# V's range and four copies of transposed probabilities on VectorE; the accumulators of the feed-forward layer copied out by ScalarE and VectorE in turn, earlier in the engines' order

## The chip, the cores and the metric

The kernel runs on one core of a Trainium2 chip. A core has five engines with instruction queues of their own: TensorE (PE; its weight loads are shown apart as PEld), VectorE (DVE), ScalarE (ACT), GpSimd (POOL) and SyncE (SP), which here issues all the DMAs. Each engine works through its queue in order and waits on semaphores for the others. SBUF is the on-chip memory; PSUM is the memory that matmuls write to. The metric is the device time of one execution in microseconds (us), given as the median of several runs.

## The reference

```python
scores = q @ k.T / sqrt(64)                      # B=4, H=8, S=768, D=64
scores += -slopes[h] * dist                      # slopes 2**-(h+1)
scores = where(keep, scores, -1e9)               # 8 global columns, or the 96 last keys
a = exp(scores - max); a /= a.sum() + 1e-9
x = (a @ v).transpose(0, 2, 1, 3).reshape(3072, 512)
h = x @ moe_w_in                                 # 512 x 2048
g = maximum(h, 0) + alpha * minimum(h, 0)        # alpha: one per column of h
out = g @ moe_w_out                              # 2048 x 512
```

q, k and v arrive as fp32, the two weight matrices as 64-bit floats; out is fp32.

## The kernel before

**Units.** The 3072 tokens are cut into 12 units of 256 tokens, three to a batch (unit u belongs to batch u // 3). `attend(u, h)` does one head of a unit: scores sp on PE, bias and maximum on DVE (pr and sm, L670), exp on ACT (L675), then the probabilities are transposed. In units 0 to 2 PE transposes them into PSUM (tp, L696) and ACT copies them to SBUF (pt, L700); in later units a DMA does it (ps to vp's layout, L720). `av` (L734) multiplies with V, and DVE writes the normalised head into xn (L743). `x_transpose` makes xt, the feed-forward layer's input, as a high and a low half-precision part.

**Feed-forward layer.** Each unit goes through 16 blocks f of 128 hidden columns. `ff_in` does h (12 matmuls of 128x256, L793), ACT scales it with alpha into g (L342), DVE takes the maximum (L814), ACT casts to the high part (L816), and POOL or DVE makes the low rest (L366). `ff_out` adds the block to two accumulators in PSUM, o_0 and o_1, 128 tokens each (3 matmuls of 128x512 for either, L831); from unit 2 on these come from a pool of two, so that the next unit's first o product into an accumulator waits until this one is emptied. After block 15 each is copied to SBUF with a scale: `os`, on ACT (L838), 128x512, and sent out by a DMA on SP (L841). Names carry the unit first: os6_1 is unit 6's second accumulator.

**V's range.** V is scaled by a power of two per batch. `v_range(b)` finds it: the batch's V is loaded in pieces (vr), the sum of absolute values of each row of 512 goes into a column of vm (6 columns; ACT, L446, one Abs with an accumulator for each 512), their maximum into vmm (L452), vdg = identity times vmm (L456), a matmul against ones spreads it over the partitions (vrow, L458), DVE takes the maximum (L460), and nine tiny instructions (L465 to L475) make vs (V's scale), vden and osc (the scale of os). For batch 0 the vr are loaded in three pieces of two rows (L438), for batches 1 to 3 in six (L444), through the two buffers of the tag "stage", which os uses too. vp, V as high and low part, is V times vs (L343 or L345 on first part, L367 on the rest), made from the loaded unit `raw`; raw's buffer is free for the next load after that.

**Weights.** In the first 125 us the weights of the 16 blocks are converted from 64-bit words and split (`wf`, `wb`, `whl`; L531 to L540 and L367), largely on DVE.

**Order.** Nothing is ordered by hand. Each operation is recorded with a key (for a block: its time slot; 16 a unit), one or more engines that may do it, with a cost in ns, and the buffers that it reads and writes. A list scheduler then plays the run through: an engine that comes free takes the ready operation of the lowest key whose buffers can be had, and an operation with several possible engines goes to a second one when the first is far behind. Buffers of one tag are handed out in the order of the keys of their first use, so one that stands later in this queue waits for those ahead of it even if a buffer is free. The tags that matter here: stage (2 buffers), wf (4), raw's four tags, o (2, PSUM). The queues that come out of it are fixed in the program.

Of the kernel before, what the change touches and what calls it, by code (L numbers as in the profile page):

```python
# [19 lines left out]
ALU = mybir.AluOpType  # L20
AX = mybir.AxisListType
PSUM = bass.MemoryType.PSUM

P = 128
# [6 lines left out]
NU = 12  # L31
# [255 lines left out]
def c_dma(nbytes):  # L287
    return nbytes / 360.0
# [5 lines left out]
VR = -23  # L294
# [28 lines left out]
def fast(tc, cn, a):  # L323
    nc = tc.nc
    ctx = ExitStack()
    with ctx:
# [7 lines left out]
        def op(eng, key, cost, fn, r=(), w=()):  # L334
            plan.op(key, r, w, (eng, cost, fn))
# [95 lines left out]
        def v_range(b, key):  # L431
            m = buf("vm", f"vm{b}", [P, 6])
            for i in range(3):

                t = [buf("w", f"vr{b}_{i}", [P, 2, 512])] * 2 if not b else [
                    buf("stage", f"vr{b}_{i}_{j}", [P, 512]) for j in range(2)]
                if not b:
                    op("SP", key, c_dma(P * 4096), lambda t=t, i=i: nc.sync.dma_start(  # L438
                        out=t[0].t, in_=a["v"][b, 2 * i : 2 * i + 2].rearrange("j p d -> p j d")), w=[t[0]])
                for j in range(2):  # L440
                    k = key + 2 * i + j if b else VR
                    x = (lambda t=t, j=j: t[j].t) if b else (lambda t=t, j=j: t[j].t[:, j, :])
                    if b:
                        op("SP", k, c_dma(P * 2048), lambda x=x, i=i, j=j: nc.sync.dma_start(  # L444
                            out=x(), in_=a["v"][b, 2 * i + j]), w=[t[j]])
                    op("ACT", k, c_act(512, ptr=1), lambda x=x, i=i, j=j: nc.scalar.activation(  # L446
                        out=x(), in_=x(), func=AF.Abs, accum_out=m.t[:, 2 * i + j : 2 * i + j + 1]),
                       r=[], w=[(t[j], j), (m, 2 * i + j)])
# [134 lines left out]
        def attend(u, h, key):  # L583
# [106 lines left out]
            if plain:  # L690
                tp = buf("ax" if u == 1 else idle(u, h, "av", "o", "o"), "tp" + uh, [P, 512])

                def transposes():
# [3 lines left out]

                op("PE", key + 2, 109 * nb, transposes, r=[pr], w=[tp])
                pt = buf(idle(u, h, "pt", "ps"), "pt" + uh, [P, 512])
                op("ACT", key + 2, c_act(npr, True), lambda: nc.scalar.copy(out=pt.t[:, :npr], in_=tp.t[:, :npr]),  # L700
                   r=[tp], w=[pt])
                prods = lambda: ((pt.t, vrt()),)
                used = [pt, rv]
                cost = 207 * nb
# [115 lines left out]
        def ff_out(u, f, key):  # L820
            gh, gl, parts = mo.pop((u, f))
            w = whl[f]
            if f == 0:
                acc[u] = [buf(("sp", "ax")[t] if u == 1 else "o", f"o{u}_{t}", [P, 512]) for t in range(2)]
            for t in range(2):
                o = acc[u][t]

                def products(t=t, o=o):
                    tok = slice(128 * t, 128 * t + 128)
                    for n, (g_, wi) in enumerate(((gh, 0), (gh, 1), (gl, 0))):  # L830
                        nc.tensor.matmul(o.t, lhsT=g_()[:, tok], rhs=w.t[:, wi, 512:1024],  # L831
                                         start=f == 0 and n == 0, stop=f == NF - 1 and n == 2)

                op("PE", key + 0.1 * t, 3 * 215.8, products, r=[*parts, (w, 1), (w, 3)], w=[o])
                if f == NF - 1:
                    s = buf("stage", f"os{u}_{t}", [P, 512])
                    by = osc[u // 3]
                    op("ACT", key, c_act(512, True, 1), lambda o=o, s=s, by=by: nc.scalar.mul(  # L838
                        out=s.t, in_=o.t, mul=by.t), r=[o, by], w=[s])
                    rows = u * UT + 128 * t  # L840
                    op("SP", key, c_dma(P * 2048), lambda s=s, rows=rows: nc.sync.dma_start(  # L841
                        out=a["out"][rows : rows + 128, :], in_=s.t), r=[s])

        def warm(key):

# [196 lines left out]
```

## Time and profile before

| what | value |
|---|---|
| runs | 657.33 us median of 3 (656.55 to 657.67) |
| profiled execution | 654.4 us, of which the span from the first to the last instruction is 652.6 |
| PE busy | 622.7 us, 95% |
| DVE busy | 516.0 us, 79% |
| ACT busy | 407.1 us, 62% |
| POOL busy | 167.6 us, 26% |
| mean granted PE clock | 0.998 |

PE and PEld overlap, and a busy PE need not be at its peak. The profile's rows give the start in us, the length in us, then engine, line and operation, the tile that is written, `<-`, and what is read, shapes as partitions x elements, and how many instructions follow one another; in square brackets the idle time of the engine just before, and what ended it. Rows of groups give busy time in us, mean ns of one, and idle time. Rows of waits give the total in us, how many there were, and the longest.

### The profile page before, as it was taken

The numbers are of one execution on the slowest core, as the hardware profiler recorded it, in microseconds if no ns is written. First come the engines' busy times: TensorE is split into PE (matmuls) and PEld (weight loads), VectorE is DVE, ScalarE is ACT, GpSimd is POOL, SyncE is SP. The second block draws the span as 40 slices with busy tenths as digits, with TensorE's granted clock in tenths as the row PEclk, the third lists the DMA queues.
The fourth block names the chain that finished last, engine by engine and source line by source line (L and its number), as shares of the span: only waits on it lengthen the run. The fifth ranks groups of instructions, "written<-read, shape, count | busy, mean of one in ns | idle before, by whom it ended". The sixth has DMA issues, their size and how long they took to land.

```text
span 652.6 us, 13802 instructions
## 1 busy us (share of the span) xinstructions
PE 622.7 (95%) x4940; PEld 442.4 (68%) x4940; DVE 516.0 (79%) x1422; ACT 407.1 (62%) x1093; POOL 167.6 (26%) x201
## 2 busy tenths in 40 slices
PE   8898989899999999899899999999999999999996
PEld 6675667576667776677677677677676777776663
DVE  6899999969779979868979878868979878844331
ACT  6897767565557666766566655675566665743432
POOL 0013434203324324303434123211532212200000
PEclk9999999999999999999999999999999999999999
DMA  8998422217546846655556566574657566311001
GB/s 298 402 408 328 138 83 83 83 35 173 174 100 124 196 110 125 168 148 139 138 144 140 152 139 140 140 164 110 171 152 135 133 162 138 84 33 33 34 1 37
DMA packets 115804, 92.86 MB, mean 142 GB/s; under 512 B 93968, under 2 KB 93968, under 8 KB 115728
## 3 DMA queue, kind: packets, MB, share of 16 engines
q1 hardware_dynamic: 115728, 91.91, 52.7%
q8 instruction: 40, 0.66, 0.4%
q14 instruction: 36, 0.29, 0.1%
HBM read 63.06 MB, written 6.29 MB: 106 GB/s over the span
## 4 chain that ended last, share of the span: by engine, by line
PE 43%; DVE 36%; DMA 9%; ACT 7%; issue 4%; POOL 0%; SPq 0%; DVEq 0%; ACTq 0%; POOLq 0%
PE o L831 18%; PE h L793 17%; DMA raw<-in_qkv_dram 8%; DVE ps L367 4%; PE sp L664 4%; DVE g L814 3%; DVE wf L537 3%; DVE wb L534 3%; DVE whl L367 3%; PE av L734 3%; DVE pr L670 3%; DVE vp L367 2%; ACT pr L675 2%; DVE wb L531 2%; DVE q L366 1%
## 5 line engine op out<-in xcount | busy, mean ns | idle before, releaser
L793 PE MATMUL h<-xt,whl 128*128 128x256 f16 x2304 | 281.7, 273 | 3.7 <-DVE g L814 2.1
L793 PEld LDWEIGHTS <-whl 128*128 128x128 f16 x2304 | 224.6, 98 | 65.6 <-issue 4.8
L831 PE MATMUL o<-whl,g 128*128 128x512 f16 x864 | 215.3, 380 | 5.1 <-ACT os L838 5.1
L831 PEld LDWEIGHTS <-g 128*128 128x128 f16 x864 | 77.8, 98 | 73.3 <-issue 7.0
L342 ACT ACTIVATE g<-h,ak 128x256 f32<-128x256 f32 x172 | 80.2, 467 | 56.7 <-PE h L793 55.4
L675 ACT ACTIVATE pr<-pr,sm 128x256 f32<-128x256 f32 (+1 forms) x192 | 93.1, 486 | 32.8 <-DVE sm L670 32.7
L814 DVE SCALAR_TENSOR_TENSOR g<-h,g 128x256 f32<-128x256 f32 x192 | 80.0, 418 | 34.9 <-ACT g L342 34.5
L816 ACT CAST g<-g 128x256 f16<-128x256 f32 x144 | 57.4, 399 | 77.1 <-DVE g L814 76.9
L670 DVE CUSTOM_DVE_ANT_0 pr<-sp,D 128x256 f32<-128x256 f32 (+1 forms) x192 | 71.5, 393 | 14.0 <-PE sp L664 13.5
L366 POOL TENSOR_TENSOR g<-g 128x256 f16<-128x256 f32 x58 | 44.3, 763 | 149.0 <-ACT g L816 141.1
L367 DVE SCALAR_TENSOR_TENSOR ps<-pr,ps 128x512 f16<-128x512 f32 (+1 forms) x72 | 61.1, 849 | 7.7 <-ACT ps L342 7.1
L366 DVE TENSOR_TENSOR g<-g 128x256 f16<-128x256 f32 x86 | 38.6, 448 | 26.1 <-ACT g L816 26.0
L366 POOL TENSOR_TENSOR gl<-g,gh 128x256 f16<-128x256 f32 x32 | 31.9, 998 | 104.6 <-ACT gh L816 94.3
L831 PE MATMUL o<-whl,gh 128*128 128x512 f16 x192 | 57.2, 380 | 0.0
L366 POOL TENSOR_TENSOR k<-raw,k 128x416 fp32r<-128x416 f32 (+1 forms) x37 | 41.0, 1108 | 52.9 <-ACT k L354 30.8
L366 POOL TENSOR_TENSOR q<-raw,q 64x256 fp32r<-64x256 f32 x42 | 34.0, 810 | 79.9 <-ACT q L354 57.8
L664 PE MATMUL sp<-k,q 128*128 128x256 f32 (+1 forms) x288 | 51.5, 301 | 2.5 <-DVE sm L670 1.6
L664 PEld LDWEIGHTS sp<-k,q 128*128 128x128 f32 x288 | 38.6, 190 | 4.9 <-issue 2.0
L367 DVE SCALAR_TENSOR_TENSOR vp<-raw,vs,vp 128x256 f16<-128x256 f32 (+1 forms) x72 | 40.7, 586 | 0.0
L831 PE MATMUL o<-whl,gl 128*128 128x512 f16 x96 | 36.4, 379 | 2.2 <-POOL gl L366 1.7
L675 ACT ACTIVATION_READ_ACCUMULATOR pr<-pr,sm 128x1 f32 x192 | 36.2, 188 | 0.0
L342 ACT ACTIVATE ps<-pr 128x512 f16<-128x512 f32 (+1 forms) x53 | 32.0, 604 | 1.4
(109 smaller groups left out, 696.0 us busy)
## 6 DMA issues: line engine op xcount, KB each, us to landing
raw<-in_qkv_dram SPq DMA_DIRECT2D x56, 464.0 KB, 3.9
w<-in_w_dram SPq DMA_DIRECT2D x32, 512.0 KB, 9.0
raw<-in_qkv_dram SPq DMA_DIRECT2D x24, 368.0 KB, 3.7
out_dram<-os SPq DMA_DIRECT2D x24, 256.0 KB, 2.3
vr<-in_v_dram SPq DMA_DIRECT2D x18, 256.0 KB, 3.8
first<-in_first_dram SPq DMA_DIRECT2D x4, 464.0 KB, 6.1
vr<-in_v_dram SPq DMA_DIRECT2D x3, 512.0 KB, 9.3
first<-in_first_dram SPq DMA_DIRECT2D x4, 336.0 KB, 9.5
```

The lines of the kernel that those rows point to most:

```text
L342: lambda: nc.scalar.mul(out=out(), in_=src(), mul=by.t if tile_ else by)),
L366: return e.tensor_tensor(out=out(), in0=src(), in1=hi(), op=ALU.subtract)
L367: return e.scalar_tensor_tensor(out=out(), in0=src(), scalar=val(), in1=hi(), op0=ALU.mult, op1=ALU.subtract)
L534: op("DVE", k, c_dve(n), lambda bits=bits, hi_=hi_: v.scalar_tensor_tensor(out=bits.t, in0=hi_(), scalar=-0x80000000, in1=bits.t, op0=ALU. ...
L537: op("DVE", k, c_dve(n), lambda w=w, bits=bits, lo_=lo_: v.scalar_tensor_tensor(out=w.t.bitcast(I32), in0=lo_(), scalar=29, in1=bits.t, op ...
L664: nc.tensor.matmul(sp.t[:, pc : pc + n], lhsT=q_()[:, 128 * qb : 128 * qb + 128], rhs=kk()[:, off : off + n], start=j == 0, stop=j == len( ...
L670: op("DVE", key, c_dve(n) + 10, lambda qb=qb, n=n, dc=dc, pc=pc: v.tensor_tensor_reduce(out=pr.t[:, pc : pc + n], in0=sp.t[:, pc : pc + n] ...
L675: op("ACT", key + 1, c_act(n, ptr=1) + 93, lambda qb=qb, n=n, pc=pc: nc.scalar.activation(out=pr.t[:, pc : pc + n], in_=pr.t[:, pc : pc + ...
L793: nc.tensor.matmul(hp.t, lhsT=w.t[:, wi, wc], rhs=x.t[:, NC * xi + c, :], start=n == 0, stop=n == 3 * NC - 1)
L814: op("DVE", key, c_dve(UT), lambda: v.scalar_tensor_tensor(out=g_(), in0=hp.t, scalar=KG, in1=g_(), op0=ALU.mult, op1=ALU.max), r=[hp], w= ...
L816: op("ACT", key, c_act(UT), lambda: nc.scalar.copy(out=gh_(), in_=g_()), r=[rg], w=[rh])
L831: nc.tensor.matmul(o.t, lhsT=g_()[:, tok], rhs=w.t[:, wi, 512:1024], start=f == 0 and n == 0, stop=f == NF - 1 and n == 2)
```

## The change

1. For batch 0 three DVE `tensor_reduce` with absolute value take the place of six ACT Abs: each reduces a loaded piece 128 x 2 x 512 into two columns of vm.
2. In unit 0, heads 4 to 7, the pt copy (128x384) is DVE's `tensor_copy` instead of ACT's.
3. os of o_0 stays on ACT, os of o_1 goes to DVE (`tensor_scalar`, 128x512 from PSUM); from unit 2 on both have a key lower by 8, eight blocks further up, and take a buffer of the tag wf instead of stage. The DMA keeps its key.
4. In unit 11, the last, each accumulator is copied in halves of 256 columns, the first by ACT and the second by DVE, with a DMA for each half.

```diff
@@ -437,12 +437,16 @@
                 if not b:
                     op("SP", key, c_dma(P * 4096), lambda t=t, i=i: nc.sync.dma_start(
                         out=t[0].t, in_=a["v"][b, 2 * i : 2 * i + 2].rearrange("j p d -> p j d")), w=[t[0]])
+                if not b:
+                    op("DVE", VR, c_dve(1024), lambda t=t, i=i: v.tensor_reduce(
+                        out=m.t[:, 2 * i : 2 * i + 2], in_=t[0].t, axis=AX.X, op=ALU.add, apply_absolute_value=True),
+                       r=[t[0]], w=[(m, i)])
+                    continue
                 for j in range(2):
-                    k = key + 2 * i + j if b else VR
-                    x = (lambda t=t, j=j: t[j].t) if b else (lambda t=t, j=j: t[j].t[:, j, :])
-                    if b:
-                        op("SP", k, c_dma(P * 2048), lambda x=x, i=i, j=j: nc.sync.dma_start(
-                            out=x(), in_=a["v"][b, 2 * i + j]), w=[t[j]])
+                    k = key + 2 * i + j
+                    x = lambda t=t, j=j: t[j].t
+                    op("SP", k, c_dma(P * 2048), lambda x=x, i=i, j=j: nc.sync.dma_start(
+                        out=x(), in_=a["v"][b, 2 * i + j]), w=[t[j]])
                     op("ACT", k, c_act(512, ptr=1), lambda x=x, i=i, j=j: nc.scalar.activation(
                         out=x(), in_=x(), func=AF.Abs, accum_out=m.t[:, 2 * i + j : 2 * i + j + 1]),
                        r=[], w=[(t[j], j), (m, 2 * i + j)])
@@ -697,8 +701,12 @@
 
                 op("PE", key + 2, 109 * nb, transposes, r=[pr], w=[tp])
                 pt = buf(idle(u, h, "pt", "ps"), "pt" + uh, [P, 512])
-                op("ACT", key + 2, c_act(npr, True), lambda: nc.scalar.copy(out=pt.t[:, :npr], in_=tp.t[:, :npr]),
-                   r=[tp], w=[pt])
+                if u == 0 and h >= 4:
+                    op("DVE", key + 2, c_dve(npr), lambda: v.tensor_copy(out=pt.t[:, :npr], in_=tp.t[:, :npr]),
+                       r=[tp], w=[pt])
+                else:
+                    op("ACT", key + 2, c_act(npr, True), lambda: nc.scalar.copy(out=pt.t[:, :npr], in_=tp.t[:, :npr]),
+                       r=[tp], w=[pt])
                 prods = lambda: ((pt.t, vrt()),)
                 used = [pt, rv]
                 cost = 207 * nb
@@ -833,13 +841,21 @@
 
                 op("PE", key + 0.1 * t, 3 * 215.8, products, r=[*parts, (w, 1), (w, 3)], w=[o])
                 if f == NF - 1:
-                    s = buf("stage", f"os{u}_{t}", [P, 512])
+                    s = buf("wf" if u > 1 else "stage", f"os{u}_{t}", [P, 512])
                     by = osc[u // 3]
-                    op("ACT", key, c_act(512, True, 1), lambda o=o, s=s, by=by: nc.scalar.mul(
-                        out=s.t, in_=o.t, mul=by.t), r=[o, by], w=[s])
                     rows = u * UT + 128 * t
-                    op("SP", key, c_dma(P * 2048), lambda s=s, rows=rows: nc.sync.dma_start(
-                        out=a["out"][rows : rows + 128, :], in_=s.t), r=[s])
+
+                    halves = (("ACT", 0, 256), ("DVE", 256, 512)) if u == NU - 1 else ((("ACT", "DVE")[t], 0, 512),)
+                    for e, lo, hi in halves:
+                        if e == "ACT":
+                            op("ACT", key - (8 if u > 1 else 0), c_act(hi - lo, True, 1), lambda o=o, s=s, by=by, lo=lo, hi=hi: nc.scalar.mul(
+                                out=s.t[:, lo:hi], in_=o.t[:, lo:hi], mul=by.t), r=[o, by], w=[(s, lo)])
+                        else:
+                            op("DVE", key - (8 if u > 1 else 0), c_dve(hi - lo, False, 1), lambda o=o, s=s, by=by, lo=lo, hi=hi: v.tensor_scalar(
+                                out=s.t[:, lo:hi], in0=o.t[:, lo:hi], scalar1=by.t, scalar2=None, op0=ALU.mult),
+                                r=[o, by], w=[(s, lo)])
+                        op("SP", key, c_dma(P * 4 * (hi - lo)), lambda s=s, rows=rows, lo=lo, hi=hi: nc.sync.dma_start(
+                            out=a["out"][rows : rows + 128, lo:hi], in_=s.t[:, lo:hi]), r=[(s, lo)])
 
         def warm(key):
 
```

Since the scheduler plays the whole run through with these operations, others change place and engine too. Up to the last weight split DVE's queue has, beside the new instructions, two 128x288 k rests fewer (POOL does them), one wf conversion fewer, two gl rests and one g more. The line numbers of the change are 4 to 16 higher than before.

The first place is DVE in unit 0, around the normalising of heads 0 to 3 (xn). Before:

```order
L684 RECIPROCAL sm0_2_267<-sm0_2_267 128x4
L743 TENSOR_TENSOR xn0_342<-av0_0_319,sm0_0_247 128x2x128
L670 ISA pr0_6_357,sm0_6_358<-sp0_6_346,D6_236 128x128
L670 ISA sm0_6_358 128x1
L670 ISA pr0_6_357,sm0_6_358<-sp0_6_346,D6_236 128x256
L670 ISA sm0_6_358 128x1
L670 ISA pr0_7_375,sm0_6_358<-sp0_7_354,D7_238 128x128
```

With the change:

```order
L441 TENSOR_REDUCE vm0_342<-vr0_0_215 128x2
L751 TENSOR_TENSOR xn0_360<-av0_0_319,sm0_0_247 128x2x128
L674 ISA pr0_6_369,sm0_6_370<-sp0_6_346,D6_236 128x128
L674 ISA sm0_6_370 128x1
L674 ISA pr0_6_369,sm0_6_370<-sp0_6_346,D6_236 128x256
L674 ISA sm0_6_370 128x1
L441 TENSOR_REDUCE vm0_342<-vr0_1_223 128x2
L751 TENSOR_TENSOR xn0_360<-av0_2_362,sm0_2_267 128x2x128
L705 COPY pt0_4_388<-tp0_4_378 128x384
L441 TENSOR_REDUCE vm0_342<-vr0_2_234 128x2
L705 COPY pt0_5_398<-tp0_5_390 128x384
L674 ISA pr0_7_402,sm0_6_370<-sp0_7_354,D7_238 128x128
```

The three reductions and the first two of the four pt copies (pt0_4, pt0_5) stand between the xn and the scores' bias and maximum of heads 6 and 7 (pr0_6, pr0_7).

The second place is the end of unit 6: g7 are blocks of unit 7, pr8 is attention of unit 8, q2_9 and k9 inputs of unit 9. Before, ACT does both copies:

```order
L816 CAST g7_1_5922<-g7_1_5922 128x256
L838 ACTIVATE os6_0_5944<-o6_0_5297,osc2_4288 128x512
L342 ACTIVATE g7_2_5953<-h7_2_5930,ak_170 128x256
L354 CAST q2_9_1_5960<-raw9_1_5874 128x256
L354 CAST k9_1_5962<-raw9_1_5874 128x288
L675 ACTIVATE pr8_5_5958,sm8_4_5887<-pr8_5_5958,sm8_4_5887 128x256
L838 ACTIVATE os6_1_5982<-o6_1_5306,osc2_4288 128x512
```

With the change ACT has only os6_0 there, in its place between the cast of block 1 and g of block 2, and DVE has os6_1:

```order
L822 SCALAR_TENSOR_TENSOR g7_1_5940<-h7_1_5914,g7_1_5940 128x256
L366 TENSOR_TENSOR g7_1_5940<-g7_1_5940 128x256
L674 ISA pr8_5_5976,sm8_4_5905<-sp8_5_5966,D5_232 128x256
L674 ISA sm8_4_5905 128x1
L822 SCALAR_TENSOR_TENSOR g7_2_5971<-h7_2_5948,g7_2_5971 128x256
L854 TENSOR_SCALAR os6_1_5998<-o6_1_5326,osc2_4483 128x512
L674 ISA pr8_5_5976,sm8_4_5905<-sp8_5_5966,D5_232 128x256
```

os6_1 moved from behind g of block 2, two casts and an exp on ACT to directly behind g of block 2 on DVE.

The third place is DVE at the V scale of batch 2, whose first unit is 6. Before, the maximum and vdg stand at block 8 of unit 4, and the scale after vrow at its block 13:

```order
L814 SCALAR_TENSOR_TENSOR g4_8_4064<-h4_8_4045,g4_8_4064 128x256
L670 ISA pr6_0_4069,sm6_0_4070<-sp6_0_4059,D0_217 128x256
L670 ISA sm6_0_4070 128x1
L452 TENSOR_REDUCE vmm2_4079<-vm2_3875 128x1
L456 TENSOR_SCALAR vdg2_4094<-ident_58,vmm2_4079 128x128
L366 TENSOR_TENSOR g4_8_4064<-g4_8_4064 128x256
L367 SCALAR_TENSOR_TENSOR ps6_0_4098<-pr6_0_4069,ps6_0_4098 128x384
```

With the change vdg stands behind os4_1, at block 2 of unit 5:

```order
L822 SCALAR_TENSOR_TENSOR g5_2_4438<-h5_2_4418,g5_2_4438 128x256
L854 TENSOR_SCALAR os4_1_4454<-o4_1_3881,osc1_2031 128x512
L460 TENSOR_SCALAR vdg2_4458<-ident_58,vmm2_2678 128x128
L822 SCALAR_TENSOR_TENSOR g5_3_4465<-h5_3_4440,g5_3_4465 128x256
L464 TENSOR_REDUCE vmm2_2678<-vrow2_4467 128x1
L469 TENSOR_SCALAR vmm2_2678<-vmm2_2678 128x1
```

and V's parts of heads 0 to 3 of unit 6 follow in one piece:

```order
L476 TENSOR_SCALAR osc2_4483<-vmm2_2678 128x1
L479 TENSOR_SCALAR osc2_4483<-osc2_4483 128x1
L343 TENSOR_SCALAR vp6_0_4122<-raw6_0_3731,vs2_173 128x192
L343 TENSOR_SCALAR vp6_1_4185<-raw6_1_3739,vs2_173 128x192
L367 SCALAR_TENSOR_TENSOR vp6_0_4122<-raw6_0_3731,vs2_173,vp6_0_4122 128x192
L367 SCALAR_TENSOR_TENSOR vp6_1_4185<-raw6_1_3739,vs2_173,vp6_1_4185 128x192
L367 SCALAR_TENSOR_TENSOR vp6_2_4286<-raw6_2_3893,vs2_173,vp6_2_4286 128x192
L367 SCALAR_TENSOR_TENSOR vp6_3_4377<-raw6_3_3912,vs2_173,vp6_3_4377 128x192
L822 SCALAR_TENSOR_TENSOR g5_4_4515<-h5_4_4490,g5_4_4515 128x256
```

The V sums and vmm of batch 2 moved up and vdg moved down, behind os4_1, with which it now shares the wf buffers; batch 3 shows the same with os7_1 and unit 9.

## The prediction

> **What bounds the kernel now.** I read the page's busy shares first, then the engines by stretches of the span, then what PE waited for.
>
> ```profile
> span 652.6 us, 13802 instructions
> PE 622.7 (95%) x4940; PEld 442.4 (68%) x4940; DVE 516.0 (79%) x1422; ACT 407.1 (62%) x1093; POOL 167.6 (26%) x201
> ...
> 0.00:25.00 25.00, 22.34 (x143) 17.59 (x144) 16.28 (x84) 19.89 (x67) 3.11 (x12) 1.00 0.92 333
> 25.00:50.00 25.00, 21.82 (x160) 17.22 (x157) 24.84 (x69) 22.97 (x59) 2.75 (x3) 1.00 1.03 407
> ...
> 100.00:125.00 25.00, 22.14 (x150) 15.25 (x148) 24.93 (x54) 18.23 (x45) 9.06 (x9) 1.00 0.22 70
> 125.00:150.00 25.00, 25.00 (x180) 18.89 (x181) 17.23 (x57) 12.13 (x37) 2.97 (x5) 1.00 0.23 62
> 300.00:350.00 50.00, 48.30 (x397) 34.18 (x396) 45.78 (x129) 31.57 (x85) 18.89 (x22) 1.00 0.58 143
> ```
>
> A row of the stretches gives the window, its length, then busy time of PE, PEld, DVE, ACT and POOL, and PE's granted clock (1.00). Three regimes show. Up to about 20 us nothing is full. From 25 to 125 us DVE is full (24.8 to 25.0 of 25) while PE is not: what is added to DVE there is paid by the end, and what is taken off is gained. From 125 us PE is full or nearly so, and only PE's idle time can be won. What ends it after 150 us:
>
> ```profile
> engine line waited for: us in total, times, longest us
> PE o L831 <- ACT os L838: 5.1, 8, 1.3
> PE h L793 <- DVE g L814: 2.1, 2, 1.4
> ```
>
> The largest is the accumulators' copy, os: the next unit's first o products wait until ACT has emptied o_0 and o_1. So the change has one clear target, worth at most 5.1 us.
>
> **The accumulators' copies.** Each of the 24 takes 0.68 us on ACT, in that engine's fixed order. The ends of units 3 and 6 show the long waits:
>
> ```profile
> 268.97 0.81 PE L831 MATMUL o<-whl,g 128*128 128x512 f16 x3 [0.41 <-ACT os L838]
> 271.03 1.46 PE L831 MATMUL o<-whl,g 128*128 128x512 f16 x6 [1.26 <-ACT os L838]
> ...
> 417.40 0.68 ACT L838 ACTIVATE os<-o,osc 128x512 f32<-128x512 f32 x1
> ...
> 418.13 0.81 PE L831 MATMUL o<-whl,g 128*128 128x512 f16 x3 [0.25 <-ACT os L838]
> ...
> 418.48 0.42 DVE L814 SCALAR_TENSOR_TENSOR g<-h,g 128x256 f32<-128x256 f32 x1 [0.18 <-ACT g L342]
> ...
> 419.47 0.68 ACT L838 ACTIVATE os<-o,osc 128x512 f32<-128x512 f32 x1
> ```
>
> The copy at 417.40 is o_0's, that at 419.47 o_1's: between them ACT does g of block 2, two casts and an exp. In unit 3 PE stood ready for o_1 at 271.03 - 1.26 = 269.77, and unit 6 repeats it with the same 1.26 us (at 420.20, so ready at 418.94). In the order of the change os6_0 keeps its place on ACT, so the waits on o_0 (0.41 and 0.25, together 0.66) stay. os6_1 goes to DVE directly behind g of block 2 (second pair of order rows), the row at 418.48, which ends at 418.90. A 512 wide copy on DVE I take at 0.68 too, like DVE's own 512 wide row (L534, below), less 0.07 of overlap: o_1 is free at about 419.5, and 1.26 becomes 0.55. Its four shorter waits, 5.1 - 0.66 - 2 x 1.26 = 1.9 us, I count as gone. Left are 0.66 + 2 x 0.55 = 1.7: **3.4 gained**. Bounds: 5.1, if the earlier places on both engines always suffice; 1.0, if DVE comes as late as ACT did but for the four short waits halved. DVE gets 13 copies more, 8.8 us over 500 us; even in its fullest 50 us after 150 it has 50 - 45.78 = 4.2 free.
>
> **V's range and the four pt copies.** They fall into unit 0:
>
> ```profile
> 18.15 0.62 ACT L446 ACTIVATE vr<-vr 128x512 f32<-128x512 f32 x1
> 18.76 0.46 ACT L700 COPY pt<-tp 128x384 f32<-128x384 f32 x1
> ...
> 12.60:20.90 8.30, 8.30 (x60) 6.47 (x59) 4.48 (x22) 8.30 (x33) 1.52 (x1) 1.00 1.03 402
> ...
> 19.83 0.55 DVE L343 TENSOR_SCALAR wf<-w 128x512 f32<-128x512 f32 x1 [0.45 <-DMA w<-in_w_dram]
> 24.16 0.68 DVE L534 SCALAR_TENSOR_TENSOR wb<-w,wb 128x512 int32<-128x512 int32 x1
> ```
>
> ACT loses six sums of 0.62 and four copies of about 0.46: 5.5 us. DVE gains three reductions of 1024 elements, which no row shows. The 256 wide g at 418.48 took 0.42 and a 512 wide wb 0.68, so 0.26 per 256 elements: 0.68 + 2 x 0.26 = 1.20, of which about 0.07 overlaps the next: 1.13 each. Half of that is the low bound, if a reduction takes two elements where these take one. [...] The four copies of 384 elements lie midway between the two rows, 0.55, or 0.47 with overlap. Together 3 x 1.13 + 4 x 0.47 = 5.3, less the wf conversion (0.55) that leaves DVE: 4.8 us more. What hides them is DVE's idle time in the stretch from 12.6 to 20.9, 8.30 - 4.48 = 3.8 us, when PE and ACT are full. Laying the change's DVE rows (first pair of order rows) out by these pitches, 3.3 of the 3.8 are used, and DVE enters the full stretch 1.5 us late; without that cover all 4.8 would be. Behind it the order takes two k rests off DVE (1.9 with overlap, row below) and adds two gl and one g (0.41 to 0.47 each, 1.0 with overlap): 1.5 - 1.9 + 1.0 = **0.6 lost**. Low bound -1.0: ACT, full in that stretch, is relieved of 5.5 us, and the exps that DVE and PE wait for come earlier. High bound 2.5: both k rests now run on POOL, beside which DVE's operations stretch, as wf's do between their least and greatest:
>
> ```profile
> L366 DVE TENSOR_TENSOR k<-raw,k 128x288 fp32r<-128x288 f32 x2 | 2.0, 984 | 0.0
> ...
> L537 DVE SCALAR_TENSOR_TENSOR wf<-w,wb x32: 659/682/1214, 26.1 to 126.5; 128x512 int32<-128x512 int32 x32
> ```
>
> [...]
>
> **The late V scale.** os now takes a wf buffer after unit 1, and vdg of batches 2 and 3 takes one of the same kind. Buffers of a kind are given out in order of keys, so vdg2 now stands behind os4_1 and vdg3 behind os7_1 (third pair of order rows): the V scale of units 6 and 9 moves from before o_0 of the last block to after it, 14 rows of PE's order later, some 17 us at 1.46 for six o products and about as much for an h. It then runs as one burst on DVE:
>
> ```profile
> 301.96 0.29 DVE L460 TENSOR_REDUCE vmm<-vrow 128x1 f32<-128x128 f32 x1
> 304.25 0.54 DVE L343 TENSOR_SCALAR vp<-raw,vs 128x192 f16<-128x192 f32 x2
> 304.71 1.39 DVE L367 SCALAR_TENSOR_TENSOR vp<-raw,vs,vp 128x192 f16<-128x192 f32 x4
> 309.39 0.30 DVE L355 CAST k<-raw 128x288 fp32r<-128x288 f32 x1
> 311.65 0.73 PE L664 MATMUL sp<-k,q 128*128 128x128 f32 x4 [0.90 <-DVE q L366]
> ...
> raw<-in_qkv_dram SPq DMA_DIRECT2D x24, 368.0 KB, 3.7
> ```
>
> From 301.96 to 304.71 + 1.39 it is 4.1 us, 3.3 without a macc maximum (0.78) between. The raw buffers come free only with vp's rests, and the next raw load lands 3.7 us later; before, the next cast came 4.7 us after the rests began and did not wait. Now DVE has little else to do ahead of that cast: laid out by the pitches it idles 1.9 us there, the next scores come 0.4 late and g of block 5 0.5: 0.9 for each of two places, less the 0.90 that PE lost at 311.65 in the old arrangement: **0.9 lost**. Bounds: 0.9 gained (no new wait, the old one gone) and, both bursts wholly in PE's way, 2 x 3.3 - 0.9 = 5.7 lost. PE's h and o of units 5 and 8 cover the rest of the burst; that cover is gone where a g that PE needs stands behind the cast on DVE. The V sums of batches 2 and 3, whose loads now need no turn behind os, move up on SP and ACT into units 2 and 3; 0.62 each on an engine with a third of its time free there: counted 0, bounds 0.6 either way, one sum ahead of an exp that PE waits for, or behind it.
>
> **The last unit.**
>
> ```profile
> 646.60 0.69 ACT os L838
> ```
>
> Only what follows PE's end at 646.58 counts. In the change DVE's half waits for ACT's half of the same accumulator, so the halves run after one another: 0.47 + 0.42 (g's 256 wide durations on ACT and DVE) against 0.69, 0.2 later, and two more DMA issues; each transfer is half as long. **0.1 lost** (-0.3 to 0.4). [...]
>
> **Sum.** -3.4 + 0.6 + 0.9 + 0.1 = -1.8. The profiled execution took 654.4 (span 652.6 and 1.8 around it) and becomes 652.6; the median of the runs, 657.33, lies 2.9 above it, so I forecast 657.3 - 1.8 = **655.5**. A measurement here can tell about 0.2% (1.3 us) from no change: faster is below 656.0, slower above 658.6.
>
> **Rivals.**
> - Even, by POOL: its k rests hold DVE up for as long as DVE is spared, and the early stretch costs 0.6 + 1.9 = 2.5. -3.4 + 2.5 + 0.9 + 0.1 = +0.1, 657.4. For it the 1214 ns maximum, against it wf's median of 682. Chance 0.17.
> - Slower, by the V scale: PE stands through both bursts. 0.6 - 3.4 + 5.7 + 0.1 = +3.0, 660.3. For it: DVE is 45.8 of 50 busy from 300 to 350, the fullest stretch after 150. Against it: the PE order places av after h of the next blocks. It decides above (3.4 - 0.6 - 0.1 + 0.9 + 1.3)/2 = 2.5 us of wait a place. Chance 0.25.
> - Better: all 5.1 go, and early stretch and V scale cost nothing: 5.0 gained, 652.3. For it ACT's 5.5 us less in unit 0. Chance 0.12.
> - The change does not do what it says: os_1 waits on DVE behind rests and casts as it did on ACT, and only 1.0 is won: -1.0 + 0.6 + 0.9 + 0.1 = +0.6, 657.9. Against it the row at 418.48. Chance 0.10.
>
> The forecast keeps 0.36. Its own range, 654 to 657, gives 0.28 to faster and 0.08 to the same; the even rival 0.03, 0.12 and 0.02; the V scale 0.25 slower; the better one 0.12 faster; the last 0.02, 0.07, 0.01. Faster 0.45, same 0.27, slower 0.28. The range runs from just under the better rival to just over the slower one: 651.5 to 661.
>
> **What would show it.** PE's waits after 150 us: os from 5.1 to about 1.7, with the 1.26s near 0.55 and DVE as releaser. DVE full from 21 rather than 25 us, reductions near 1.2 us, end of the full stretch 0.6 later. At units 6 and 9 a DVE idle near 2 us before a cast, PE waits below 1. In the end the second os half after 647.3. Wrong would be reductions of 0.7, PE waits of over 2.5 us at the V scale, or a DVE that is no longer full before 125 us.

## The result, and the profile after

The changed kernel takes 676.73 us (median of 4 runs, 675.50 to 679.47) against 656.94 for the kernel before: a ratio of 1.0315 with a 95% interval of 1.0279 to 1.0352. The forecast was 655.5 in a range of 651.5 to 661: faster was forecast, slower is what came. The ratios, here and below, leave out the most disturbed runs; medians count all. The page's head after:

```profile
span 677.6 us, 13831 instructions
PE 637.4 (94%) x4940; PEld 446.5 (66%) x4940; DVE 526.0 (78%) x1441; ACT 396.5 (59%) x1061; POOL 178.4 (26%) x207
```

PE is "busy" for 14.7 us more with the same 4940 matmuls. The stretches of the span show the larger part of why; the last three numbers are PE's granted clock, the DMA share and GB/s:

```profile
20.65:24.06 3.41, 1.85 (x16) 1.37 (x13) 3.13 (x18) 2.90 (x8) 0.00 (x0) 1.00 1.04 396
24.06:34.30 10.24, 10.12 (x41) 7.45 (x41) 8.46 (x25) 5.81 (x16) 0.00 (x0) 0.50 1.03 407
...
65.02:68.43 3.41, 3.41 (x17) 2.22 (x16) 3.41 (x8) 0.93 (x2) 3.41 (x1) 0.50 0.94 313
...
123.05:129.87 6.82, 6.82 (x23) 3.78 (x23) 5.36 (x14) 3.42 (x12) 1.40 (x2) 0.50 0.21 58
```

PE ran at half its clock for 10.24, 3.41 and 6.82 us, half of which, 10.2 us, is by my estimate the most that this can add (four sp matmuls of 64x256 at 29.57 us took 2.07 us; in the kernel before four of that shape, at 26.33, 1.13). The kernel before had a clock of 1.00 throughout the stretches shown in the prediction. Ahead of the first of these stretches PE was busy for 1.85 of 3.41 us (before, in the same window: 2.98). Its longest wait there is for the last of the four pt copies, that of head 7, which stands on DVE behind the nine small instructions of the V scale (the last of the nine is the first row):

```profile
22.77 0.15 DVE L479 TENSOR_SCALAR osc<-osc 128x1 f32<-128x1 f32 x1
22.84 0.55 DVE L705 COPY pt<-tp 128x384 f32<-128x384 f32 x1
...
23.44 2.29 PE L742 MATMUL av<-first,pt 128*128 128x64 f32 x12 [1.45 <-DVE pt L705]
```

Ahead of the other two PE waits 2.14 us for a gl and 2.56 us for a maximum sm; the kernel before waits 1.75 and 2.08 us at those places and keeps its clock. The three half-clock stretches of this trace are 3, 1 and 2 times 3.41 us long. After 150 us the waits of PE are these (columns as in the prediction):

```profile
PE h L801 <- DVE g L822: 6.4, 8, 1.4
PE sp L668 <- DVE sm L674: 2.5, 3, 1.6
PE o L839 <- DVE os L854: 2.3, 3, 0.8
PE o L839 <- ACT gh L824: 1.7, 2, 1.0
PE o L839 <- DVE gl L366: 1.7, 2, 1.0
PE sp L668 <- ACT g L342: 1.5, 2, 0.7
PE o L839 <- ACT os L851: 1.1, 2, 0.9
```

The waits for os fell from 5.1 to 2.3 + 1.1 = 3.4, by half of what was forecast (the 5.1 is itself the least of eleven traces, see below). Those for g rose from 2.1 to 6.4, and waits for gh and for sp behind g, which the list of before does not have, came in.

To place the loss I lined the two traces up by the work that PE had done (matmuls weighted with their durations). After 150 us the change is 8.2 us behind, at 240 us 11.9, at 350 us 12.2, at 450 us 16.9, at the last matmul 24.1; the end adds 0.9. So there are four losses: the first stretch, units 2 and 3, the units around the late V scales, and the end. These places are read from one execution of each. Laid over the kernel before in the same way, g4_halves (below), in which PE has the same instructions in the same order, loses 4.0 us between 150 and 640 us at full clock, and k1_before_fill 3.5; so a loss of 3 or 4 us in one trace is not yet the change's, and what each part costs is taken from the runs below.

### The profile page after: what moved, and what is told of

Same layout as the page of the kernel before. It is cut to its first block, busy times and chain, and to the rows that moved or that the text cites. A ratio compares the mean times of both kernels' runs of the same rounds, so it can differ in the third digit from the quotient of the medians.

```text
span 677.6 us, 13831 instructions
## 1 busy us (share of the span) xinstructions
PE 637.4 (94%) x4940; PEld 446.5 (66%) x4940; DVE 526.0 (78%) x1441; ACT 396.5 (59%) x1061; POOL 178.4 (26%) x207
## 4 chain that ended last, share of the span: by engine, by line
PE 39%; DVE 31%; DMA 14%; ACT 8%; issue 5%; POOL 1%; SPq 1%; ACTq 0%; DVEq 0%; POOLq 0%
PE h L801 17%; PE o L839 16%; DMA raw<-in_qkv_dram 11%; DVE ps L367 4%; PE sp L668 3%; DVE vp L367 3%; DVE g L822 3%; DVE pr L674 3%; ACT pr L679 2%; PE av L742 2%; DVE k L366 1%; DVE wb L538 1%; DVE q L366 1%; DVE vp L343 1%; DVE wf L541 1%
## 5 line engine op out<-in xcount | busy, mean ns | idle before, releaser
L801 PE MATMUL h<-xt,whl 128*128 128x256 f16 x2304 | 285.2, 275 | 8.1 <-DVE g L822 6.4
L366 POOL TENSOR_TENSOR g<-g 128x256 f16<-128x256 f32 x59 | 42.1, 713 | 189.3 <-ACT g L824 188.7
L366 POOL TENSOR_TENSOR gl<-g,gh 128x256 f16<-128x256 f32 x30 | 33.3, 1111 | 122.3 <-ACT gh L824 115.9
L366 POOL TENSOR_TENSOR k<-raw,k 128x416 fp32r<-128x416 f32 (+1 forms) x45 | 50.2, 1115 | 47.5 <-ACT k L354 22.6
L367 DVE SCALAR_TENSOR_TENSOR ps<-pr,ps 128x512 f16<-128x512 f32 (+1 forms) x72 | 55.2, 767 | 7.6 <-ACT ps L342 7.3
L366 DVE TENSOR_TENSOR g<-g 128x256 f16<-128x256 f32 x85 | 41.4, 489 | 24.0 <-ACT g L824 23.8
L366 POOL TENSOR_TENSOR q<-raw,q 64x256 fp32r<-64x256 f32 x44 | 37.5, 853 | 76.3 <-ACT q L354 42.9
L742 PEld LDWEIGHTS <-vp 128*128 128x128 f16 x792 | 27.9, 98 | 5.7
```

Of the source, the lines that this page charges most:

```text
L366: return e.tensor_tensor(out=out(), in0=src(), in1=hi(), op=ALU.subtract)
L367: return e.scalar_tensor_tensor(out=out(), in0=src(), scalar=val(), in1=hi(), op0=ALU.mult, op1=ALU.subtract)
L742: nc.tensor.matmul(out, lhsT=p_[:, 128 * j : 128 * j + 128], rhs=v_[:, 64 * j : 64 * j + 64], start=m == 0, stop=m == len(ps) - 1)
L801: nc.tensor.matmul(hp.t, lhsT=w.t[:, wi, wc], rhs=x.t[:, NC * xi + c, :], start=n == 0, stop=n == 3 * NC - 1)
```

## The experiments

**How they are compared.** The kernel before, run 91 times beside these experiments on five chips, was granted a mean clock between 0.972 and 0.999 (median 0.993), from run to run of the same program, and took 653.4 to 672.5 us. Its time follows the clock: 653.6 + 567 x (1 - clock), correlation 0.94, 1.6 us of scatter about that line. So beside each median and ratio stands the excess, the mean distance of a kernel's runs from this line at their own clocks: what it loses apart from the clock.

| run | median us | ratio, 95% interval | clock, median (range) | excess us |
|---|---|---|---|---|
| the change | 676.7 | 1.0315 (1.0279-1.0352) | 0.984 (0.983-0.986) | 14.6 |
| e1_vrange | 661.4 | - | 0.984 (0.969-0.997) | -1.1 |
| e2_copies | 657.0 | 0.9987 (0.9951-1.0023) | 0.994 (0.963-0.998) | -1.7 |
| e4_same_order | 665.3 | 1.0112 (1.0045-1.0179) | 0.978 (0.974-0.987) | -0.3 |
| h1_both | 662.8 | 1.0079 (1.0044-1.0115) | 0.984 (0.965-0.990) | 0.7 |
| h2_both_45 | 658.0 | 1.0007 (0.9976-1.0037) | 0.992 (0.973-0.997) | 0.1 |
| c1_fill | 679.3 | 1.0339 (1.0282-1.0397) | 0.990 (0.979-0.994) | 19.4 |
| k3_fill | 667.2 | 1.0189 (1.0140-1.0238) | 0.986 (0.978-0.993) | 6.8 |
| k4_fill6 | 665.3 | 1.0132 (1.0098-1.0166) | 0.988 (0.983-0.994) | 5.7 |
| k1_before_fill | 665.0 | 1.0130 (1.0092-1.0167) | 0.994 (0.986-0.998) | 7.2 |
| k2_copies_fill | 662.0 | 1.0074 (1.0043-1.0105) | 0.992 (0.987-0.998) | 4.0 |
| e3_outs | 673.9 | 1.0285 (1.0195-1.0376) | 0.984 (0.971-0.996) | 11.7 |
| f1_gate_own | 661.7 | 1.0078 (1.0048-1.0108) | 0.991 (0.985-0.996) | 3.1 |
| f2_gate | 668.1 | 1.0155 (1.0096-1.0214) | 0.995 (0.973-0.996) | 10.1 |
| f3_own | 664.5 | 1.0139 (1.0072-1.0205) | 0.990 (0.987-0.996) | 6.4 |
| g1_same_order | 663.9 | 1.0035 (1.0005-1.0065) | 0.990 (0.970-0.999) | 3.5 |
| g4_halves | 659.0 | 1.0002 (0.9975-1.0030) | 0.992 (0.970-0.999) | 0.6 |

The standard error of an excess is 0.2 to 1.0 us, and on the five chips the kernel before itself lies between -0.5 and 0.6 us from the line, so an excess below 1 us is hardly told from none. e1_vrange and e2_copies are the first and second part of the change alone, e3_outs the third and fourth, each by the scheduler.

**The first stretch: each part alone.**

> Only V's range of batch 0 on VectorE (three reductions instead of six ScalarE sums), all else as before. Clock theory (the loss before 160 us is TensorE at half its clock, set off by the idle of 1.45 us before av of heads 6 and 7, whose pt copies stand behind the V scale on VectorE): pt stays on ScalarE here, so no such idle; mean granted clock 0.998, -1 to +1 us against before. Load theory (VectorE has 4.8 us more to do in a stretch that it bounds): three reductions are 3.4 us, some of it in gaps: +1 to +3 us at the full clock.

> Only the four pt copies of unit 0 on VectorE. Clock theory: the copies of heads 6 and 7 stand behind V's scale, TensorE idles over 1 us near 22 us, a half-clock stretch of 3.4 to 10 us follows near 24 us; mean clock 0.985 to 0.992, +4 to +8 us, nearly all of it before 160 us. Load theory: 1.9 us more on VectorE, +1 to +2 us at a clock of 0.998.

Neither part loses anything at equal clock (-1.1 and -1.7): no sign of the 0.6 that I charged to DVE. e1_vrange had two runs at a clock of 0.997 and two at 0.97, 14 us apart, so its median says little. e2_copies kept before's clock, though PE waits 1.19 us there too: the clock theory's 4 to 8 us did not come, its trace has one half-clock stretch of 3.4 us at 24 us.

**The same in before's order.** The plan keeps the operations as ScalarE's; only what is emitted changes:

```diff
-lambda: nc.scalar.copy(out=pt.t[:, :npr], in_=tp.t[:, :npr])
+lambda: (v.tensor_copy if u == 0 and h >= 4 else nc.scalar.copy)(out=pt.t[:, :npr], in_=tp.t[:, :npr])
```

> V's range and the four copies both on VectorE, but every instruction of the kernel in the place of the queue order of before (the scheduler still plans them as ScalarE's). If the loss before 160 us comes from the instructions' new engine: +5 to +9 us, as in the whole change by that time, with the clock theory putting a half-clock stretch of at least 3.4 us into it and the load theory none. If it came from the scheduler's new order: within 1 us of before.

+8 us at the median, all of it clock (0.978, excess -0.3). Three of its four runs were granted 0.979 or less, as against 15 of the 91 of the kernel before at 0.980 or less: as far as four runs show it, the engine of the instructions brings the loss, not their new order. Its trace does not show how. PE waits 1.45 us for a pt copy from 19.2 to 20.7 us and 0.88 up to 25.8, but the clock is half from 19.8 to 47.1 us, so it fell 0.6 us into the first wait. And f2_gate and g1_same_order, whose unit 0 is that of before, and h2_both_45 have such a stretch of 27 to 31 us as well, from 7.8, 8.5 and 11.3 us, ahead of any of these copies.

**Which copies.** h1_both is both first parts by the scheduler; h2_both_45 leaves the copies of heads 6 and 7 on ACT:

```diff
-                if u == 0 and h >= 4:
+                if u == 0 and 4 <= h < 6:
```

> V's range and all four pt copies on VectorE, placed by the scheduler; the accumulators as before. This is the whole change's unit 0. Clock theory: the idle of about 1.45 us before av of heads 6 and 7 (their copies stand behind V's nine scale instructions) brings a half-clock stretch near 24 us in most runs: mean clock 0.983 to 0.990, +4 to +9 us against before, and the whole change minus the accumulators' part. Load theory: 0 to +2 us at a clock as before's (0.99 to 0.998).

> As the run before, but the copies of heads 6 and 7 stay on ScalarE: VectorE still has the three reductions and two copies (4.3 of the 5.3 us). Clock theory: no idle over 0.5 us at av of heads 6 and 7, a clock as before's (median 0.99 or more), -2 to +1 us against before. Load theory: 80% of whatever the run with all four loses.

This separates them. With all four copies no run of 12 was granted more than 0.990, as 58 of the 91 of the kernel before were; with two, the clock is that of before (median 0.992, 8 of 13 above 0.990) and the ratio 1.0007, though DVE has the three reductions and two of the copies. Load on DVE would have left 80% of the loss. Since e2_copies, which has all four copies but not the reductions, keeps before's clock (0.994), it takes the two together.

**Filling the idle time.** If PE's idleness ahead of av halves its clock, idle matmuls there should prevent it. They go into the bank that av then overwrites:

```diff
+                def fill():
+                    if u == 0 and h == 7:
+                        for _ in range(12):
+                            nc.tensor.matmul(av.t[:, :P], lhsT=ident, rhs=ident, start=True, stop=True)
```

> The whole change, and 12 idle matmuls of 128x128 on TensorE ahead of av of heads 6 and 7 of unit 0, into the bank that av then overwrites: they run in the 1.45 us in which TensorE waits for the pt copies, and leave every queue's order as in the change. Clock theory (that idle time sets off the half clock from 24 to 34 us): no half-clock stretch near 24 us, 3 to 6 us less than the change (671 to 674), mean clock 0.988 or more. Load theory: as the change, 676 to 677 us, since nothing that VectorE does is altered.

> The first two parts of the change (range and all four copies on VectorE), with 12 idle matmuls on TensorE ahead of av of heads 6 and 7, where it waits 1.45 us; nothing else differs from the run with both parts, which took 662.8 us at a median clock of 0.984 and never over 0.990. Clock theory: median clock 0.990 to 0.996, 656 to 660 us. Load theory (VectorE's added work, whatever TensorE does): 662 to 663 us.

> As the run with 12 idle matmuls ahead of av of heads 6 and 7, but with six: each took 0.224 us (two passes), so the 12 held TensorE up for 1.4 us beyond the wait that they were to fill; six take 1.34 us and fit into the 1.45 us. Clock theory: no time added to TensorE, median clock 0.988 or more and some runs above 0.990 (the run without them: 0.984, never above 0.990), 657 to 661 us against its 662.8. Load theory: 662 to 664 us and the same clocks as without them.

c1_fill puts 12 into the whole change, k3_fill 12 and k4_fill6 six into h1_both. The windows of h1_both, then of k4_fill6:

```profile
16.40:23.20 6.80, 5.24 (x36) 3.95 (x34) 6.49 (x31) 4.69 (x13) 0.00 (x0) 1.00 1.03 396
23.20:30.00 6.80, 6.80 (x30) 5.45 (x29) 4.74 (x17) 2.73 (x10) 0.00 (x0) 0.50 1.03 407
```

```profile
24.10:34.30 10.20, 8.26 (x64) 6.89 (x64) 9.99 (x30) 7.42 (x21) 0.00 (x0) 1.00 1.03 407
62.20:65.60 3.40, 3.40 (x19) 2.39 (x18) 3.40 (x8) 1.19 (x3) 3.40 (x1) 0.51 0.93 308
```

The stretch near 24 us is gone in all three traces, and the clock's median rises (h1_both 0.984; k3_fill 0.986, k4_fill6 0.988; c1_fill 0.990 against the change's 0.984), by less than was expected of k3_fill (0.990 to 0.996). But the clock then falls at later waits, in k3_fill already at 31 us, here at 62 us, in c1_fill at 579 us after a wait of 2.13 us, and the time got no shorter: 12 matmuls take 2.68 us (in k3_fill's trace 24 records, two each, of 0.112), more than the wait, and even six, which fit, cost 5 us of excess over h1_both. So the idle time is shown to bring the clock down at that place, as far as three single traces show it; that curing it gives the time back is not shown, and what the excess of the idle matmuls consists of stays open.

Nor does a wait alone decide what follows it. In the kernel before and in g4_halves, with the same instructions of PE, stands the same wait of 2.24 us:

```profile
29.70 0.66 PE L696 MATMUL tp<-ident,pr 128*128 128x128 f32 x4 [2.24 <-DVE xt L367]
```

```profile
28.98 1.11 PE L696 MATMUL tp<-ident,pr 128*128 128x128 f32 x4 [2.24 <-DVE xt L367]
```

The first trace keeps its full clock; in g4_halves the clock is half from 28.3 to 31.7 us. What decides between the two is not shown here. It is why the clock has to be read over many runs.

The same idle matmuls for the kernel before, with four ahead of the transposes of heads 0 to 3, and for e2_copies with both kinds:

> The kernel before, with four idle matmuls ahead of the transposes of heads 0 to 3 of unit 0 (about 6 to 13 us), 0.43 us each. Clock theory: the runs of before at a clock of 0.973 to 0.98 (8 of 35, 10 to 14 us longer) come from half-clock stretches of 27 us that begin at 8 to 11 us; with less idle time there they become rarer, 0 to 2 of 12, and the median falls by 0 to 2 us although TensorE has 1.7 us more to do. Without that link: as many slow clocks, and 0 to +2 us.

> The four copies on VectorE alone (657.0 us), with both kinds of idle matmuls, six ahead of av of heads 6 and 7. Clock theory: median clock 0.995 or more, 653 to 656 us, under before. Without that link: 657 to 659 us.

k1_before_fill had no run below 0.986 in 6 (before: 15 of 91 at 0.980 or less, so one such run would be expected), but lost 8 us, of which its 16 idle matmuls are 16 x 0.22 = 3.5; the rest stays open. PE was busy for 8.30 of 8.30 us in a row of the prediction's from this unit: what is put in there is paid. No version beats the kernel before; e2_copies is nearest and not distinguishable from it.

**The accumulators' part alone.**

> Only the accumulators' copies (ScalarE and VectorE, key lower by 8, wf buffers, last unit in halves); unit 0 as before. If the 16 us lost after 150 us come from this part (late V scale at units 6 and 9, later raw loads): +12 to +17 us with a clock of 0.998 and the first 150 us as before. If they follow from the late first stretch: -2 to +2 us.

The third and fourth part alone have an excess of 11.7 of the change's 14.6, with the first 150 us as before (-0.3 us in the trace) and a clock of 1.00 until PE's last matmul in its profiled execution: the loss after 150 us is this part's own.

**V's work put back.** In f1_gate_own both moves of V's work that the new buffers brought are undone, in f2_gate only the early sums, in f3_own only the late scale:

```diff
+                           r=[osb[3 * b - 3]] if b > 1 and i == j == 0 else [], w=[t[j]])   # f1, f2
-            dg = buf("wf", f"vdg{b}", [P, 3, P])
+            dg = buf("vdg" if b > 1 else "wf", f"vdg{b}", [P, 3, P])                       # f1, f3
```

> The accumulators' part of the change alone, with V's work of batches 2 and 3 put back in its old place: the first V load of a batch waits for the last os of the batch's first unit less three, as it did by the stage buffers, and vdg has a buffer of its own. Theory V (the 14 us of the accumulators' part come from V's sums in units 2 and 3 and from the late V scale, both moved by the change of buffers, not from copying on VectorE): 0 to -4 us against before, the loss between 150 and 240 us and the steps at units 6 and 9 gone. Rival (os on VectorE, eight blocks earlier, delays g and the casts): still +8 to +14 us.

> As the accumulators' part alone, but only V's sums held back to their old place; vdg still takes a wf buffer behind os, so the V scale stays late. Theory V: the 5 us between 150 and 240 us are gone, the steps at units 6 and 9 stay: +5 to +9 us against before. Rival: +8 to +14.

> As the accumulators' part alone, but only vdg in a buffer of its own; V's sums of batches 2 and 3 stay early, in units 2 and 3. Theory V: 4 to 5 us lost between 150 and 240 us, no step at units 6 and 9: +2 to +6 us against before. Rival: +8 to +14.

Excesses 3.1, 10.1 and 6.4. Added to f1_gate_own, the late V scale costs 10.1 - 3.1 = 7.0 and the early sums 6.4 - 3.1 = 3.3; with f1's 3.1 that is 13.4, beside e3_outs' 11.7 (standard error 0.9). Taken away from e3_outs they cost less, 11.7 - 6.4 = 5.3 and 11.7 - 10.1 = 1.6; each of these differences has a standard error of 0.7 to 1.2. Most of the loss is V's, as that theory had it, but f1_gate_own is not at 0 to -4: the copies' part loses even with V's work in place. How the early sums cost, in e3_outs, unit 2:

```profile
190.42 0.63 ACT L446 ACTIVATE vr<-vr 128x512 f32<-128x512 f32 x1 [3.60 <-DMA vr<-in_v_dram]
...
193.38 0.61 PE L831 MATMUL o<-whl,gh 128*128 128x512 f16 x2 [2.15 <-ACT gh L816]
```

ACT stands 3.60 us for a V load, and behind the sum in its queue stand casts, an exp and gh, for which PE waits 2.15. In the kernel before these sums ran at 274 to 287 and 424 to 438 us, here from 173 to 215. The late scale of unit 6 in the change, DVE, then SP, then PE:

```profile
330.32 1.40 DVE L367 SCALAR_TENSOR_TENSOR vp<-raw,vs,vp 128x192 f16<-128x192 f32 x4
...
334.44 0.29 DVE L355 CAST q<-raw 128x256 fp32r<-128x256 f32 x1 [1.50 <-DMA raw<-in_qkv_dram]
...
330.79 11.66 SPq L615 DMA_DIRECT2D raw<-in_qkv_dram  x7
342.59 3.51 SPq L728 DMA_TRANSPOSE vp<-ps  x2
...
336.18 0.70 PE L668 MATMUL sp<-k,q 128*128 128x128 f32 x4 [0.38 <-DVE q L366]
340.05 0.70 PE L668 MATMUL sp<-k,q 128*128 128x128 f32 x4 [0.73 <-ACT g L342]
341.86 0.70 PE L668 MATMUL sp<-k,q 128*128 128x128 f32 x4 [0.45 <-DVE sm L674]
345.79 1.47 PE L801 MATMUL h<-xt,whl 128*128 128x256 f16 x12 [0.72 <-DVE g L822]
```

The rests free the raw buffers, seven loads go out in one piece (before: five, 9.52 us from 305.18), DVE waits 1.50 for the first and then has the casts, rests and scores of all of unit 6's remaining heads at once; PE waits four times, 2.3 us. Unit 9 repeats it (2.2). SP, in order, holds the next probabilities' transposes back until 342.59.

**os on DVE in before's order.**

```diff
-                    op("ACT", key, c_act(512, True, 1), lambda o=o, s=s, by=by: nc.scalar.mul(
+                    op("ACT", key, c_act(512, True, 1), lambda o=o, s=s, by=by, t=t: v.tensor_scalar(... ) if t else nc.scalar.mul(
```

> Every instruction in the place of the queue order of before, os_1 of each unit emitted on VectorE instead of ScalarE, nothing else. If VectorE is the better place for os_1 (as the forecast took it): PE's waits for os fall from 5.1 to 2 us or less, -2 to -4 us. If VectorE's queue is as late there as ScalarE's (it is 80% busy against 62%): waits for os 4 to 6 us, time within 1.5 us of before.

PE's waits for os, in g1_same_order for DVE's alone, in f1_gate_own, and the copies' durations in the change (min/median/max in ns, with the last unit's halves):

```profile
PE o L831 <- DVE os L838: 7.5, 6, 1.7
```

```profile
PE o L834 <- DVE os L850: 5.7, 5, 2.3
```

```profile
L851 ACT ACTIVATE os<-o,osc x13: 474/682/687, 170.0 to 670.7; 128x512 f32<-128x512 f32 x11, 128x256 f32<-128x256 f32 x2
L854 DVE TENSOR_SCALAR os<-o,osc x13: 482/743/751, 170.5 to 671.2; 128x512 f32<-128x512 f32 x11, 128x256 f32<-128x256 f32 x2
```

The 5.1 of the kernel before is the least of eleven traces whose accumulators are copied as before (the others: 5.7 to 7.5). g1_same_order in the old order, with 1.0 for ACT's copies beside its 7.5, waits longer than all of them. f1_gate_own, in the new order with V's work in place, lies among them with 5.7; the forecast's 1.7 is far from both. In the latter, units 3 to 7:

```profile
273.67 0.59 PE L834 MATMUL o<-whl,g 128*128 128x512 f16 x2 [0.70 <-DVE os L850]
324.33 0.59 PE L834 MATMUL o<-whl,g 128*128 128x512 f16 x2 [1.04 <-DVE os L850]
374.89 0.59 PE L834 MATMUL o<-whl,g 128*128 128x512 f16 x2 [2.34 <-DVE os L850]
424.44 0.38 PE L834 MATMUL o<-whl,g 128*128 128x512 f16 x1 [0.68 <-DVE os L850]
473.76 0.59 PE L834 MATMUL o<-whl,g 128*128 128x512 f16 x2 [0.95 <-DVE os L850]
```

The long waits of units 3 and 6, which are 1.25 or 1.26 in all eleven traces with the old copies, became 0.70 and 0.68, near the forecast's 0.55. Those of units 4, 5 and 7, which the forecast counted as gone, are 1.04, 2.34 and 0.95 (before 0.80, 0.40 and 0.50; at most 0.81, 1.96 and 0.92 in the eleven). f3_own repeats them with 1.04, 2.19 and 1.03. In unit 5 it is DVE's own queue that is late:

```profile
369.97 0.30 DVE L355 CAST q<-raw 128x256 fp32r<-128x256 f32 x1 [1.76 <-DMA raw<-in_qkv_dram]
...
370.76 1.51 DVE L367 SCALAR_TENSOR_TENSOR ps<-pr,ps 128x512 f16<-128x512 f32 x1
...
374.09 0.74 DVE L850 TENSOR_SCALAR os<-o,osc 128x512 f32<-128x512 f32 x1
```

It waits 1.76 us for a load and only then comes to the rests that stand ahead of the copy. The copy itself is longer too (743 against 682 ns). Why the change, with 3.4, waits less for os than f1_gate_own was not taken apart; its PE comes to the accumulators later. Another wait came with the new order: in all six traces that have it PE waits 1.7 us after 150 us for gl on DVE, against 0.4 to 0.8 in the eleven and 0.4 in g1_same_order. With it and the end, f1_gate_own's loss of 3.1 is the size of what PE waits more than before, 12.1 against 10.1 us after 150, and 0.9 at the end; but in five of the eleven traces PE's waits also sum to 13.0 to 13.6, so one trace does not prove the sum.

**The last unit in halves.**

> Only the last unit's copies in halves, ScalarE then VectorE, with four DMAs; all else as before. If the issue of the DMAs on SP sets the end (0.45 us each, one behind the other): the span ends 6.9 to 7.2 us after TensorE's last matmul rather than 6.0, +0.9 to +1.2 us. By the forecast: +0.1.

The end of the queue on SP, in the kernel before and in the change:

```profile
646.67 0.98 SPq L841 DMA_DIRECT2D out_dram<-os  x2
```

```profile
671.09 1.79 SPq L857 DMA_DIRECT2D out_dram<-os  x4
```

The last issue ends 1.08 us after PE's last matmul before, 2.20 in the change and 2.35 in g4_halves, and the span's end moves from 6.05 to 6.91 and 7.23. So 0.9 to 1.2 as expected; in the ratio (1.0002) it is lost in the scatter.

## Why the prediction was wrong

- **The early stretch (0.6 lost, -1.0 to 2.5).** The sizes were right: the reductions took 1.21 to 1.22 us (forecast 1.20), the copies 0.55 (0.55), and PE did lose nothing to DVE's load (h1_both and h2_both_45 at equal clock 0.7 and 0.1). The step that failed stands before the sum: "PE's granted clock (1.00)" was read as a property of the kernel. It was one execution's; the kernel before itself varies from 0.972 to 0.999, and the change sits at 0.984. (0.993 - 0.984) x 567 = 5 us of the 20 are this. The order of the change puts the last pt copy behind V's scale instructions; I laid the rows out for DVE's lateness, without asking what PE does meanwhile. That the two parts together lower the clock is shown by the runs (h1_both against h2_both_45); that PE's wait is how rests on single traces.
- **The late V scale (0.9 lost, up to 5.7).** The largest miss. The right place and mechanism, and the rival that the forecast gave 0.25, but mis-sized. The 1.9 us of idle DVE was 1.50; the PE waits behind it were 2.3 and 2.2 us a place instead of 0.9. I followed the first cast only, not the burst of seven loads and the casts behind them, nor SP, where the transposes wait. Measured: 5.3 to 7.0 us by the two differences, at the bound of 5.7 or above it. The four waits at each place sum to 4.5 us, against the 0.90 before; that the rest is the attention work pushed back, which comes due in the following units, is argued from the waits for g there (6.4 against 2.1) and not tested.
- **The V sums moved into units 2 and 3 (0, -0.6 to 0.6).** Above its bound of 0.6, by the two differences: 1.6 to 3.3 us. I priced the sum's 0.62 us on ACT, not ACT's wait for the load (3.60 us) with gh behind it. The step moved DMAs, and their landing belonged to its price.
- **The accumulators' copies (3.4 gained, 1.0 to 5.1).** Wrong in sign: f1_gate_own loses 3.1 with these copies, 0.6 of it the last unit's (by g4_halves' excess; 0.9 to 1.2 in the traces). The two waits of 1.26 did fall, by about as much as forecast. The step that failed is "Its four shorter waits ... I count as gone": three of them grew, to 4.3 us together, in f1_gate_own and in f3_own. In unit 5 the trace shows why: the copy on DVE stands behind that engine's casts and rests, and so behind the loads for which they wait. The 1.7 us for gl was no term of the sum at all. The key lower by eight left os6_0 where it was, as the order rows showed (it "keeps its place"), so that copy was not eight blocks earlier.
- **The last unit (0.1 lost, to 0.4).** The halves run after one another as forecast (0.47 and 0.48; forecast 0.47 and 0.42). What was left out is the issue: four DMAs at about 0.45 us one behind the other on SP, 0.9 to 1.2 in all.
- **The rivals.** "Slower, by the V scale" was the nearest, at 660.3; its price left out the clock (5), the early sums (1.6 to 3.3), the os copies and the end. "Even, by POOL" rests on a stretching of DVE beside POOL that the trace of before shows only in part: eight of its 32 wf conversions took 0.88 to 1.21 us, each beside work of POOL, but four others (59.05, 59.66, 103.25, 118.29 us) were beside it for 0.38 us or more and took 0.66 to 0.68. That the 1.9 us come back in full is shown by no run: in e1_vrange and e2_copies POOL does four of those rests up to 130 us against two before, and they lose nothing at equal clock.

At equal clock the pieces 7.0 + 3.3 + 3.1 (with the end) + 0.7 (h1_both) give 14.1 beside the measured 14.6, and 5 more are the clock. With e3_outs' measured 11.7 in place of the first three it is 12.4, so the agreement is within about 2 us.

## What to carry to other kernels

Where buffers of one kind are handed out in the order of keys, giving an operation another buffer moves every other user of both kinds: look for who had been held back by the old one (here loads that then came 100 to 220 us early) and who stands behind in the new one. In the trace of the change, waits of TensorE of 1.45, 2.14 and 2.56 us were followed by 10.24, 3.41 and 6.82 us at half the clock, while the 2.24 us of the kernel before were followed by full clock; so in a stretch with such waits ask for each moved instruction whether TensorE stands still behind it, and compare kernels at equal clock, over several runs, before blaming an engine. Two waits came back to the hundredth in eleven traces (1.25 or 1.26 us), a shorter one did not (0.29 to 1.96 in unit 5): look at several traces before a short wait is counted as gain. Two DMAs that were cut in two cost two issues more on their queue, about 0.45 us each, and at the end of this kernel they were on the path: 0.9 to 1.2 us.

## What the runs showed of the hardware

The mean clock granted to one unchanged one-core program varied from 0.972 to 0.999 over 91 runs on five chips, and its time follows it (correlation 0.94): 567 us for each unit of clock, about 0.43 us for each microsecond at half speed in a span of 657. The four traces with a mean clock of 0.972 to 0.974 (e4_same_order, f2_gate, g1_same_order, h2_both_45) each have one stretch of 27 to 31 us at half speed that begins between 7.8 and 19.8 us. A reduction with absolute value of 128x1024 elements took 1.21 to 1.22 us on VectorE; a copy of a 128x512 accumulator with a scale 743 ns on VectorE and 682 on ScalarE. An idle 128x128 fp32 matmul of the identity with itself stands in the trace of k3_fill as two records, 0.112 us each (12 matmuls, 24 records, 2.68 us).
